# A backward pass of a gated spectral/GEGLU block: the real DFT over d split into even and odd d, joined and parted at the spectral filter

## The chip, the cores and the metric

One core of one Trainium2 chip. The metric is device time of one execution in microseconds (us). The kernel before takes 1464.88 us, the median of three runs (1464.13 to 1465.75).

## The reference, cut to what matters

S = 2048 rows, D = 576 columns, F = 4608, bf16 throughout. The kernel computes the forward output and all gradients of

```python
g = sigmoid((x * gate_w).sum(-1, keepdims=True))
a = irfft2(rfft2(x) * (w_r + 1j * w_i))                  # over (S, D): 2048 x 289 spectrum
b = (gelu(x @ w_gate) * (x @ w_up)) @ w_down
out = g * a + (1 - g) * b
# outputs: out, and d(out) . grad_out for x, w_r, w_i, w_gate, w_up, w_down, gate_w
```

So one 2-D real DFT is taken of x and one of g * grad_out; with W = w_r + i w_i the spectra give X W (for a), G conj(W) (for dx) and G conj(X) (for dw_r, dw_i); the first two are transformed back. The DFT over d gives 289 values of l for each row, each a sum over 576 d of x times cos and sin.

## The kernel before, in words

Everything that a DFT does is a matmul against a table of cosines and sines.

*Stage 0, the head* (before the loop over g). x and grad_out are loaded, transposed on TensorE in chunks (`tchunk`, L268 to 286) into xT and dOT (d on the partitions, five chunks: four of 128 d and one of 64). `build_D` (L95) makes the tables Dt: for each chunk of 128 d, cos and sin for all 289 l. `build_R` and `build_B` make the tables for the two halves of the DFT over s (2048 = 16 x 128). `fwd_units` (L476) gives 16 units u1 (over d: ten matmuls of 289 columns, L483, then an eviction by ACT, L487 or L489) and 16 units u2 (first half over s: four matmuls, L497 to L500, an eviction by DVE or ACT, L503/L505, a store). For x all 32 run in the head, on four PSUM tiles in turn; `gate` (L288) ends it.

*Stage 1, the loop over g* (18 blocks of 256 columns of F) and m (4 blocks of 512 rows): 72 steps. Each step runs `H_mm` (z = dO w_down^T, L312/L315; xy = x [w_gate w_up], L319/L324), the elementwise GEGLU and its derivative (`H_da`, `H_q`, `H_ew1`, `H_ew2`: ACT evicts and takes sigmoids, DVE does 24 operations per step on 128x512 bf16 tiles), and stores three results A, dHg, dHu to DRAM on SP's queue (L383). Between them stand the weight-gradient matmuls of the block g before (`W_units`, L417, L434, L447), evicted by `wevac`: every third by DVE, the others by ACT. `load_w` loads the next block's weights, one part at the end of each of the first three steps.

The rest of the spectral branch is a list `fft` of 174 slots, spread over the steps by `want` (L768): 4 slots in each of the first four steps, then 2.59 per step, evenly. The list: u1/u2 for grad_out; the filter stage `mid_units` (L535); two inverse transforms `inv_units` (L648). In the filter stage 16 rows i are taken in pairs p. s2 (L547) finishes the DFT over s: four matmuls and one ACT eviction into X or G. Then `products` (L569) puts DVE operations into the list `side`: two halvings, six products of 1156 elements (L583) and six sums and differences of 578 (L589/L590); three items of `side` are issued after each of a step's two elementwise tiles. s1 (L615) starts the way back: four matmuls, one ACT eviction, two stores. In `inv_units` z and ztail do the second half over s, d (L691) the transform over l: per row i and for cos and sin, two matmuls of 289 columns against Dt and one against the small table At2 for the last 33 l (L698, L700); ACT evicts, and DVE gives columns d from the sum and 576 - d from the difference of the two (L704, L705).

All spectral units in the loop share one PSUM tile with z (`pftile`, tag "z", one buffer). All small tiles (Y, Vt, Vp, W, X, G, products, ev, yo) share one pool of 19 buffers (`unit`).

*Stage 2*: the matmuls over F (L945) for b and dx, from A, dHg, dHu transposed back by DMA, with `post` and `x_end` on DVE; `gate_grad` (L988) sums dlog x over the 2048 rows by 80 one-column matmuls (L993).

The order of every engine's work is that in which the code issues it. SP's queue issues all loads and most stores in order; POOL's issues the stores of weight gradients from two `stage` buffers.

Of the kernel before, what the change touches and what calls it, by code (L numbers as in the profile page):

```python
# [9 lines left out]
ACT = mybir.ActivationFunctionType  # L10
# [30 lines left out]
NL = DF - 256  # L41
# [16 lines left out]
def iotas(nc, res, unit):  # L58
# [3 lines left out]
    tb.lrow = unit([DF], F32, name="lrow")  # L62
    G.iota(tb.lrow[:], pattern=[[1, DF]], base=0, channel_multiplier=0, **kw)
    tb.dcol = res.tile([P, 5], F32, name="dcol")
    G.iota(tb.dcol[:, 0:4], pattern=[[128, 4]], base=0, channel_multiplier=1, **kw)
# [10 lines left out]
    G.iota(tb.qcol_i[:], pattern=[[0, 1]], base=0, channel_multiplier=1)  # L76
    tb.halfpi = res.tile([P, 1], F32, name="halfpi")
# [17 lines left out]
def build_D(nc, tb, unit, res, c0, n):  # L95

    V = nc.vector
    step = 2.0 * math.pi / D
    TS = (nc.gpsimd if c0 else V).tensor_scalar
    X = unit([n, DF], F32, name="XD")  # L100
    y = unit([n, DF], F32, name="yD")
# [6 lines left out]
    o = unit([n, 2, DF], name="Dt")  # L108
    V.scalar_tensor_tensor(y[:], X[:], -1.0, X[:], op0=ALU.mult, op1=ALU.max)
    r = LO if c0 == 4 else slice(0, P)  # L110
    if c0 == 4:
        nc.gpsimd.memset(o[HI, :, :, :], 0.0)
    nc.scalar.activation(o[r, :, 0, :], y[r], ACT.Sin, bias=tb.halfpi[r], scale=-step)
    nc.scalar.activation(o[r, :, 1, :], X[r], ACT.Sin, scale=-step * EPS_SCALE)
    tb.Dt += [o[:, c] for c in range(n)]
# [51 lines left out]
def kernel(  # L167
# [25 lines left out]
    scr_x = dram.tile([T, P, 2, DF], BF16, name="scr_x")  # L193
    scr_g = dram.tile([T, P, 2, DF], BF16, name="scr_g")
    scr_p1 = (dram.tile([T, P, 2, 256], BF16, name="scr_p1"), dram.tile([2, T, P, NL], BF16, name="scr_q1"))
    scr_p2 = (dram.tile([T, P, 2, 256], BF16, name="scr_p2"), dram.tile([2, T, P, NL], BF16, name="scr_q2"))
# [7 lines left out]
    wts = {}  # L204

    def load_w(g, part):

        fsl = slice(g * FG, (g + 1) * FG)
        if part == 0:
            wgu = wpool.tile([P, 5, 2 * FG], BF16, tag="wgu", name="wgu")  # L210
            wdT = wpool.tile([P, 5, FG], BF16, tag="wdT", name="wdT")
            wts[g] = wgu, wdT
        wgu, wdT = wts[g]
        if part < 2:
            w, cols = (B_w_gate, B_w_up)[part], slice(part * FG, (part + 1) * FG)
            LD.dma_start(wgu[:, 0:4, cols], w[0:512, fsl].rearrange("(c p) f -> p c f", p=P))
            for r in (LO, HI):
                LD.dma_start(wgu[r, 4, cols], w[512:D, fsl])
# [127 lines left out]
    def H_ew1(xy, q):  # L346
# [6 lines left out]
        V.tensor_tensor(q[:], xb[:], q[:], op=ALU.mult)  # L353
        return xb, q, s, hu

    stores = []

    def flush(n=9):

# [735 lines left out]
```

## Time and profile before

| What | Value |
|---|---|
| median of three runs | 1464.88 us |
| profiled execution | 1460.16 us, span 1458.4 us, mean granted clock 0.997 |
| PE matmul / weight load | 1440.9 us / 1065.9 us |
| DVE, ACT, POOL | 845.7, 686.0, 120.3 us |
| head | 0 to 51.8 us |
| loop over g and m | 51.8 to about 1004 us, 72 steps |
| filter stage, s2 and s1 | 221 to 561 us |
| inverse transforms | 578 to 910 us |
| PE stops and waits | 10 us in all, 4.9 of them for the first load of x |

In a line of the profile, L312 is line 312 of the kernel; "out<-in" are tiles by the program's names; 128*128 128x289 is a matmul of 128x128 weights that writes 128 partitions by 289 columns. A matmul's own time includes the filling of the array, so its cost is read from the distance between the starts of two that follow each other. A stretch of the table of stretches gives, after its bounds and length, the busy time of each engine with the number of instructions, then the granted clock, the DMA engines' mean busy share and GB/s.

### The profile page before, as it was taken

The page shows a single profiled execution, that of the slowest core. Times are in us where ns is not written, and L with a number is a line of the kernel's source. Part 1 is how long each engine was busy: PE and PEld are TensorE (multiplying, and loading weights), DVE is VectorE, ACT ScalarE, POOL GpSimd, SP SyncE. Part 2 cuts the span into 40 slices and gives each one's busy share as a digit, 9 for nine tenths or more (in the row PEclk, how much of TensorE's full clock was granted, in tenths as well). Part 3 has the DMA queues.
Part 4 walks back from the last instruction along what each step waited for, and adds up shares of the span by engine and source line. Part 5 has one row for each costly group of instructions (what it writes and reads, how often), then busy time and mean ns, then how long its engine had stood idle before and what let it go on. Part 6 is the DMA issues. An engine that isn't in the chain of part 4 may idle for free.

```text
span 1458.4 us, 30071 instructions
## 1 busy us (share of the span) xinstructions
PE 1440.9 (99%) x11776; PEld 1065.9 (73%) x11776; DVE 845.7 (58%) x2256; ACT 686.0 (47%) x1354; POOL 120.3 (8%) x206
## 2 busy tenths in 40 slices
PE   8999999999999999999999999999999999999998
PEld 6766677767777677677677677768877777777776
DVE  7697677888887886777777777773000531212100
ACT  5776666766676666766766766662000000000000
POOL 2000011001011001001001001100000100000000
PEclk9999999999999999999999999999999999999998
DMA  5244344455445445434543544757999998878773
GB/s 192 68 122 120 115 130 120 137 146 143 138 139 150 117 119 138 125 110 113 143 127 102 139 127 118 176 135 172 255 197 198 218 198 166 165 159 169 149 149 72
DMA packets 501160, 210.54 MB, mean 144 GB/s; under 512 B 320950, under 2 KB 491128, under 8 KB 501016
## 3 DMA queue, kind: packets, MB, share of 16 engines
q1 hardware_dynamic: 491416, 188.10, 54.4%
q0 software_dynamic: 7792, 19.49, 4.3%
q8 instruction: 92, 1.51, 0.5%
q10 hardware_dynamic: 1808, 1.02, 0.3%
q14 instruction: 52, 0.43, 0.1%
HBM read 40.89 MB, written 93.82 MB: 92 GB/s over the span
## 4 chain that ended last, share of the span: by engine, by line
PE 92%; DVE 4%; ACT 1%; issue 1%; DMA 0%; DVEq 0%; ACTq 0%
PE acc L945 29%; PE wps L434 17%; PE xy L324 16%; PE wps L417 9%; PE z L312 8%; PE wps L447 2%; PE xy L319 2%; PE z L315 1%; PE pf L698 1%; PE pf L672 1%; PE pf L483 1%; PE pf L700 1%; PE fx L483 0%; DVE Vt L503 0%; DMA pin<-scr 0%
## 5 line engine op out<-in xcount | busy, mean ns | idle before, releaser
L945 PEld LDWEIGHTS <-pin 128*128 128x128 bf16 x3456 | 338.8, 98 | 87.0 <-DMA pin<-scr 1.0
L324 PE MATMUL xy<-wgu,xT 128*128 128x512 bf16 x1152 | 271.4, 380 | 0.0
L434 PEld LDWEIGHTS <-xn 128*128 128x128 bf16 x2304 | 225.3, 98 | 32.4 <-issue 0.2
L324 PEld LDWEIGHTS <-xT 128*128 128x128 bf16 x1152 | 106.8, 98 | 137.4 <-issue 30.4
L337 ACT ACTIVATE da<-z,omg 128x256 bf16<-128x256 f32 x288 | 113.4, 475 | 147.7 <-PE z L315 144.6
L962 ACT COPY bo<-acc 128x288 f32<-128x288 f32 x32 | 12.8, 399 | 308.9 <-PE acc L945 308.9
L417 PE MATMUL wps<-dB,A 128*128 128x288 bf16 x1152 | 154.2, 286 | 0.0
L945 PE MATMUL acc<-wgT,pin 128*128 128x288 bf16 x1152 | 145.3, 288 | 0.0
L945 PE MATMUL acc<-wuT,pin 128*128 128x288 bf16 x1152 | 143.6, 286 | 0.0
L945 PE MATMUL acc<-wd_all,pin 128*128 128x288 bf16 x1152 | 142.8, 286 | 0.7 <-DMA pin<-scr 0.7
L312 PE MATMUL z<-wdT,dOT 128*128 128x256 bf16 x1152 | 137.7, 273 | 1.7 <-ACT Y L489 1.2
L417 PEld LDWEIGHTS <-A 128*128 128x128 bf16 x1152 | 112.7, 98 | 35.7
L434 PE MATMUL wps<-dHg,xn 128*128 128x256 bf16 x1152 | 134.4, 273 | 0.0
L434 PE MATMUL wps<-dHu,xn 128*128 128x256 bf16 x1152 | 131.5, 273 | 0.0
L312 PEld LDWEIGHTS <-dOT 128*128 128x128 bf16 x1152 | 111.2, 98 | 19.1 <-issue 6.0
L1019 DVE SCALAR_TENSOR_TENSOR f32t<-gwf,dlog,b16t 128x576 f32<-128x576 f32 x16 | 13.1, 817 | 185.9 <-DMA b16t<-dxa_scr 185.9
L343 ACT ACTIVATE q<-xy 128x512 bf16<-128x512 f32 x144 | 86.1, 598 | 70.1 <-PE xy L324 65.8
L367 ACT ACTIVATE om<-s 128x512 bf16<-128x512 bf16 x144 | 92.0, 639 | 9.1 <-DVE s L351 8.9
L350 DVE TENSOR_SCALAR s<-q 128x512 bf16<-128x512 bf16 x144 | 42.8, 298 | 90.5 <-ACT q L343 88.4
L368 ACT ACTIVATE s<-s 128x512 bf16<-128x512 bf16 x144 | 90.7, 630 | 4.6
L440 POOL DMA_DIRECT2D out_dram<-dw x67 | 48.3, 721 | 534.3 <-ACT dw L395 256.7
L349 ACT CAST hu<-xy 128x512 bf16<-128x512 f32 x144 | 87.0, 604 | 0.0
(187 smaller groups left out, 1771.5 us busy)
## 6 DMA issues: line engine op xcount, KB each, us to landing
scr<-A SPq DMA_DIRECT2D x144, 128.0 KB, 2.2
scr<-dHg SPq DMA_DIRECT2D x144, 128.0 KB, 2.0
scr<-dHu SPq DMA_DIRECT2D x144, 128.0 KB, 2.1
out_dram<-dw POOLq DMA_DIRECT2D x67, 128.0 KB, 2.6
wd_all<-in_B_w_down_dram SPq DMA_DIRECT2D x3, 1728.0 KB, 15.0
out_dram<-dwd POOLq DMA_DIRECT2D x34, 144.0 KB, 2.2
wgu<-in_B_w_gate_dram SPq DMA_DIRECT2D x18, 256.0 KB, 3.1
wgu<-in_B_w_up_dram SPq DMA_DIRECT2D x18, 256.0 KB, 3.1
```

The costliest lines, as they stand in the source:

```text
L312: nc.tensor.matmul(zo(t), lhsT=dOT[:, ci, t, :], rhs=wdT[:, ci, :], start=(t % 4 < 2 and ci == 0), stop=False)
L324: nc.tensor.matmul(xy[k][:, t % 2, :], lhsT=xT[:, ci, t, :], rhs=wgu[:, ci, :], start=False, stop=(ci == 3))
L337: nc.scalar.activation(da[:, tt, :], z[:, tt, k, :], ACT.Copy, scale=omg32[:, t:t + 1])
L343: nc.scalar.activation(q[:], xy[:, :, 0:FG], ACT.Square)
L349: nc.scalar.copy(hu[:], xy[:, :, FG:2 * FG])
L350: V.tensor_scalar(s[:], q[:], A_GELU, 1.0, op0=ALU.mult, op1=ALU.add)
L367: nc.scalar.activation(om[:], s[:], ACT.Sigmoid, scale=-2.0 * C_GELU)
L368: nc.scalar.activation(s[:], s[:], ACT.Sigmoid, scale=2.0 * C_GELU)
L417: nc.tensor.matmul(wps[:, :288], lhsT=tl(0, t)[:, fch * P:(fch + 1) * P], rhs=dB[:, t, h * 288:(h + 1) * 288], start=(t == 0), stop=(t == ...
L434: nc.tensor.matmul(wps[:, cc, :], lhsT=xn[:, t, (c0 + cc) * P:(c0 + cc + 1) * P], rhs=tl(k, t), start=(t == 0), stop=(t == T - 1))
L440: wst[0].dma_start(ov[:, c0:c0 + TPB, fsl], dw[:])
L945: nc.tensor.matmul(acc[:, :288], lhsT=src[:, r, :], rhs=w_of(r)[:, h * 288:(h + 1) * 288], start=(first and r == 0), stop=(last and r == F ...
```

## The change

Since cos and sin of 2 pi l d / 576 keep their value or change their sign when l goes to l + 288, according to whether d is even or odd, an even and an odd sum over l = 0 .. 144 hold what 289 values held: with e and o the two, value l is e + o and value 288 - l comes from e - o (its imaginary part with the sign turned, and for row -k of the spectrum). The change carries every spectrum in that form up to the filter and from it.

- The transposes take every second column of d; tables have 145 columns (HF) instead of 289; u1 has six matmuls of 290 columns (even, odd, and one chunk of 64 d for both) instead of ten of 289. u2, s2, s1 keep four matmuls, of 290 columns.
- In s2 ACT evicts to f32 (`xe`), and two DVE operations of 290 and 288 elements write e + o and e - o, the latter backwards, into X and G.
- Since the second half of each spectrum row stands at row -k, w_r and w_i are copied in DRAM with their rows reversed (34 copies on POOL's queue at the end of the head, from DRAM to DRAM, 2 x 128 rows of 144 bytes each), POOL negates w_i's half, and the gradients of w are written to DRAM and copied back reversed (34 copies on SP's queue, three per step, after the last pair).
- `fold` turns each product back into e and o (four DVE operations of 576 elements per pair, half of them with a reversed input, and two small copies). The scaling by SD2 moves into `gs32`.
- d has, for cos and sin, two matmuls of 145 columns and one of 290; the table for odd d on the way back (`Oi`) is made by transposes in `tail_table`.
- `want` counts a slot of the filter stage as 1.7; while in that stage, `wevac` leaves DVE out. The A tiles have 13 buffers instead of 14.
- `load_w` loads w_gate and w_up in part 0, transposes w_down to `wtmp` in part 1 and copies it into wdT in the new order of d in part 2 (four more copies).
- `gate_grad`: DVE accumulates dlog x over the row blocks, and ten one-column matmuls remain.

```diff
+HF = 145
+NL = 2 * (HF - P)
+def eo(c):
+    return slice(256 * (c % 2) + c // 2, 256 * (c % 2) + 256, 2)
...
         elif part == 1:
+            wtmp[0] = wpool.tile([P, 4, FG], BF16, tag="wtmp", name="wtmp", bufs=1)
+            LD.dma_start_transpose(wts[g][1][:, 4:5, :], B_w_down[fsl, DCH[4][0]:D])
+            LD.dma_start_transpose(wtmp[0][:], B_w_down[fsl, 0:512])
         else:
+            wdT = wts[g][1]
             LD.dma_start(wdT[LO, 4, :], wdT[HI, 4, :])
+            for par in range(2):
+                for h, r in enumerate((LO, HI)):
+                    LD.dma_start(wdT[r, 2 * par:2 * par + 2, :], wtmp[0][par:P:2, h:4:2, :])
...
-    keepA = wstack.enter_context(tc.tile_pool(name="keepA", bufs=14))
+    keepA = wstack.enter_context(tc.tile_pool(name="keepA", bufs=13))
...
-                        nc.tensor.transpose(tp_[:, 0, j, tt, :], src[:, t0 + tt, c * P:(c + 1) * P], ident[:])
+                        nc.tensor.transpose(tp_[:, 0, j, tt, :], src[:, t0 + tt, eo(c)], ident[:])
...
-        if ectr[0] % 3 == 0:
+        if ectr[0] % 3 == 0 and not in_mid[0]:
             V.tensor_copy(out, in_)
...
-                for c, ci in [(c, ci) for c in range(2) for ci in range(4)] + [(0, 4), (1, 4)]:
-                    nc.tensor.matmul(yps[:, c, :DF], lhsT=src[:, ci, t, :], rhs=tb.Dt[ci][:, c, :],
-                                     start=(ci == 0), stop=(ci == 4))
+                for par, j in [(par, j) for par in range(2) for j in range(2)] + [(0, 2), (1, 2)]:
+                    ci, tab = (4, 4 + par) if j == 2 else (2 * par + j, 2 * par + j)
+                    nc.tensor.matmul(yps[:, par, :2 * HF], lhsT=src[:, ci, t, :], rhs=tb.Dt[tab].rearrange("p c l -> p (c l)"),
+                                     start=(j == 0), stop=(j == 2))
...
+    def reversed_rows(eng, src, dst):
+        s_, d_ = (a.rearrange("(m i) (h l) -> h i m l", i=T, h=2) for a in (src, dst))
+        return [lambda i=i: eng.dma_start(d_[:, i], s_[:, T - i, ::-1]) for i in range(1, T)] + \
+            [lambda: eng.dma_start(d_[:, 0, 1:P], s_[:, 0, P - 1:0:-1]), lambda: eng.dma_start(dst[0:1], src[0:1])]
...
-            LD.dma_start(w[:, 0], wr_v[:, i0:i0 + 2, :])
-            LD.dma_start(w[:, 1], wi_v[:, i0:i0 + 2, :])
+            for k, v in enumerate((wr_v, wi_v)):
+                LD.dma_start(w[:, k, :, 0:HF], v[:, i0:i0 + 2, 0:HF])
+                LD.dma_start(w[:, k, :, HF:DF], tiles_of(wrev[k])[:, i0:i0 + 2, :])
+            nc.gpsimd.tensor_scalar(w[:, 1, :, HF:DF], w[:, 1, :, HF:DF], -1.0, None, op0=ALU.mult)
...
-                if which == "x":
-                    nc.scalar.copy(o[:, ii], xps[:, :, :DF])
-                else:
-                    nc.scalar.activation(o[:, ii], xps[:, :, :DF], ACT.Copy, scale=SD2)
+                xe = unit([2, 2 * HF], F32, name="xe")
+                nc.scalar.copy(xe[:], xps[:, :, :w])
+                V.tensor_tensor(o[:, ii, :, 0:HF], xe[:, :, 0:HF], xe[:, :, HF:w], op=ALU.add)
+                V.tensor_tensor(o[:, ii, :, DF - 1:HF - 1:-1], xe[:, :, 0:HF - 1], xe[:, :, HF:w - 1], op=ALU.subtract)
...
+            def fold(key):
+                def f():
+                    m = st[p, key]
+                    q = unit([2, 2, 2, HF], name="q" + key)
+                    for e, op in enumerate((ALU.add, ALU.subtract)):
+                        V.tensor_tensor(q[:, :, :, e, 0:HF - 1], m[:, :, :, 0:HF - 1], m[:, :, :, DF - 1:HF - 1:-1], op=op)
+                    V.tensor_copy(q[:, :, :, :, HF - 1], m[:, :, :, HF - 1:HF].to_broadcast([P, 2, 2, 2]))
+                    st[p, key + "_q"] = q
+                return f
...
                 def store():
+                    for k, v in enumerate((o2v, o3v)):
+                        LD.dma_start(v[:, i0:i0 + 2, 0:HF], o[:, :, k, 0:HF])
+                        LD.dma_start(tiles_of(orev[k])[:, i0:i0 + 2, :], o[:, :, k, HF:DF])
+                    if p == T // 2 - 1:
+                        for k, v in enumerate((out_2, out_3)):
+                            moves.extend(reversed_rows(LD, orev[k][:], v[:, HF:DF]))
...
-                LD.dma_start(dst[0][i], Vt[:, :, 0:256])
-                LD.dma_start(dst[1][:, i].rearrange("c p l -> p c l"), Vt[:, :, 256:DF])
+                LD.dma_start(dst[0][i].rearrange("p c (e l) -> p c e l", e=2), Vt[:, :, :, 0:P])
+                for c in range(2):
+                    LD.dma_start(dst[1][c, i], Vt[:, c, :, P:HF])
...
                 for c in range(2):
-                    for lc in range(2):
-                        nc.tensor.matmul(yps[:, c, :DF], lhsT=Z[:, ii, 2 * lc + c, :], rhs=tb.Dt[lc][:, c, :],
-                                         start=(lc == 0), stop=False)
+                    for e, tab in enumerate((tb.Dt[0], tb.Oi)):
+                        nc.tensor.matmul(yps[:, c, e * HF:(e + 1) * HF], lhsT=Z[:, ii, 2 * e + c, :], rhs=tab[:, c, :],
+                                         start=(e == 0), stop=False)
...
+    for k, v in enumerate((A_w_r, A_w_i)):
+        for move in reversed_rows(nc.gpsimd, v[:, HF:DF], wrev[k][:]):
+            move()
...
+        def load(n):
+            return n + 0.7 * min(max(n - mid_at, 0), n_mid)
...
+            for _ in range(3):
+                if moves:
+                    moves.pop(0)()
...
+            V.scalar_tensor_tensor(gacc[:], xn[:, t, :], dlog[:, t:t + 1], gacc[:], op0=ALU.mult, op1=ALU.add)
...
-                for t in range(T):
-                    nc.tensor.matmul(gps[0:n, c:c + 1], lhsT=xn[:, t, c * P:c * P + n], rhs=dlog_bf[:, t:t + 1],
-                                     start=(t == 0), stop=(t == T - 1))
+                for v in range(2):
+                    nc.tensor.matmul(gps[0:n, c:c + 1], lhsT=gsplit[:, v, c * P:c * P + n], rhs=ones[:],
+                                     start=(v == 0), stop=(v == 1))
```

## The prediction

> **What bounds the kernel now.** I read the busy shares first, then the chain of work that ended last, then the table of stretches, then PE's timeline for the pace of one matmul. Busy shares and chain:
>
> ```profile
> PE 1440.9 (99%) x11776; PEld 1065.9 (73%) x11776; DVE 845.7 (58%) x2256; ACT 686.0 (47%) x1354; POOL 120.3 (8%) x206
> PE 92%; DVE 4%; ACT 1%; issue 1%; DMA 0%; DVEq 0%; ACTq 0%
> ```
>
> TensorE is busy 99% of the span and is 92% of the chain. "PE busy" is an extent and not a pace, so the table of stretches has to confirm it. Its columns are the stretch, its length, then busy PE, PEld, DVE, ACT, POOL:
>
> ```profile
> 11.10:49.80 38.70, 38.08 (x385) 29.85 (x386) 25.71 (x60) 25.45 (x42) 0.00 (x0) 1.00 0.38 115
> 63.40:94.20 30.80, 29.39 (x200) 17.85 (x200) 28.77 (x78) 25.69 (x49) 0.00 (x0) 1.00 0.47 133
> 94.20:122.50 28.30, 27.29 (x224) 19.22 (x224) 26.90 (x80) 19.84 (x38) 1.81 (x3) 1.00 0.36 102
> 252.80:570.60 317.80, 317.62 (x2539) 225.63 (x2538) 267.72 (x707) 215.54 (x430) 30.57 (x48) 1.00 0.50 137
> 1104.00:1430.00 326.00, 325.96 (x2661) 260.39 (x2662) 72.20 (x169) 7.99 (x20) 24.21 (x44) 1.00 0.86 173
> ```
>
> See three things. From 122 us on PE never rests. VectorE has much room in the last stage, 16% room in the filter stage (252.8 to 570.6 us, where spectra are multiplied), and almost none from 63 to 122 us. There PE does lose time: 0.8 us of z waiting for ACT's Y, 0.9 us of L483 waiting for DVE's Vt. So a matmul removed is time removed, except where DVE is already full.
>
> **Prices on PE**, from its timeline (start, extent, line):
>
> ```profile
> 15.93 1.05 PE L275 MATMUL tp<-ident,xn 128*128 128x128 bf16 x16
> 16.92 0.41 PE L278 MATMUL tp<-ident,xn 128*64 128x128 bf16 x8
> ...
> 21.24 1.40 PE L483 MATMUL fx<-Dt,xT 128*128 128x289 bf16 x10
> 22.48 0.28 PE L497 MATMUL fx<-Y,Rt 128*128 128x289 bf16 x1
> ...
> 49.77 2.14 PE L292 MATMUL fx<-gwT,xT 128*128 128x1 bf16 x80
> 51.77 1.91 PE L312 MATMUL z<-wdT,dOT 128*128 128x256 bf16 x16
> ...
> 902.52 0.41 PE L698 MATMUL pf<-Dt,ZT 128*128 128x289 bf16 x2
> 902.77 0.29 PE L700 MATMUL pf<-At,ZU 66*128 66x289 bf16 x1
> ```
>
> Start to start: ten matmuls of 289 columns take 1.24 us, 124 ns each; sixteen of 128 columns 0.99 us, 62 ns; eighty of one column 2.00 us, 25 ns. The last shows that a weight load costs at most 25 ns of pace, so halving the columns does halve a matmul.
>
> **What goes from PE.** (a) u1, forward over d: 10 matmuls become 6, in 32 units: 32 x 4 x 0.124 = 15.9 us, half of it in the head (before 49.8 us), half in 56 to 171 us. (b) d, inverse: four of its six matmuls go from 289 to 145 columns. 145 columns cost 62 ns (half of 124) to 70 ns (62 x 145/128); I take 64: 32 x 4 x 0.060 = 7.7 us. (c) gate_grad: 80 one-column matmuls become 10, priced like L292: 1.75 us. Back: one column more on some 600 matmuls (0.4 ns each, 0.25 us) and eight transposes in tail_table (0.4 us). **Sum: 24.7 us.** The head's transposes now load every second column; even at double the 25 ns, that load stays under the 62 ns pace.
>
> **What is added, and what covers it.**
>
> *DVE in the filter stage.* Per pair p (8 slots): s2 now unfolds on DVE, 8 tensor_tensors of 290 f32, like L704 (458 ns): 3.7 us. fold adds twice two bf16 tensor_tensors of 576, one input of one of them read backwards, and a copy of 8 (0.17). No row reads bf16 backwards; the bounds are L589 (578 bf16, 460 ns) and L979 (576 f32, 752 ns): 2.2 to 3.4 us. The products remain: by their rows 7.65 us. So 7.65 becomes 13.5 to 14.7. A plain step (the last four, 948.5 to 995.5 us) has 9.05 us of DVE, a step of the filter stage 267.72/24 = 11.15 in 13.24, thus 2.1 us of products per step, at 2.59 slots per step 6.5 us per pair: overlap makes it 85% of the rows' sum. The new want() gives the stage 2.0 slots a step (4 steps per pair) and moves the wevac third (0.45 us a step) to ACT: 8.6 + 14.7 x 0.85/4 = 11.7 us of DVE in a step that PE needs 12.9 for (0.6 slots of 0.5 us fewer): 91%, against 84%. Two steps in four are heavier: products come six a step, so some 13 us against 12.4. The q, s, hu and da buffers of two and three tiles let DVE trail by most of a step, and step 291.8 to 306.7 had DVE at 14.14 of 14.90 with PE at 14.76. I charge 2 us (0 to 10). ACT takes those evictions at 9.0 of 13.2 us (an f32 eviction, L703, costs 653 ns, the bf16 one, L560, 643): covered.
> Two waits are new on DVE. The unfold waits for ACT's copy of s2; behind it stand sig1's tile and ACT's sigmoids of it, and DVE waits there only when it is ahead. With 13 A buffers the second tile of m = 2 waits for PE's dwd reads of the g before; behind it stand dHg and dHu. DVE runs that tile after PE has passed, so nothing; without that cover 1 us in each of 17 g.
> The Trainium skill, "VectorE: DVE Perf Modes", section "Mode 2×_1P — pack two bf16 into one 32-bit read", grants two results a cycle at a step of +1 or -1, with 4-byte alignment. L589 and L590 disagree on the alignment: rows starting at 578 bytes run as fast. By that page fold stands, as an estimate, at 2.2 us per pair, and the 2 us charged become about 1.
>
> *The head.* PE's 38.08 us fall to about 30.2, DVE's 25.7 and ACT's 25.5 stay (83%); u2 waits for ACT's Y with 1.24 us of PE work between instead of 1.74, and one copy behind one sine is 0.64 + 0.62. I charge 1 us (0 to 3), 1 us for the tail_table copies ahead of the gate (0 to 2), and credit 0.5 for half-width tables. In the last stage 16 ops like L976 (818 ns) are nothing: DVE has 72 busy of 326 us.
>
> *63 to 122 us.* DVE had 55.7 of 59.1 us and loses nothing; u1 would save 4 to 5 us there, 3.4 is all the room. Charge 2.5 us (0.5 to 4.5).
>
> *Denser slots outside the filter stage*, 3.4 instead of 2.59 a step through the one z bank: the four-slot steps lost 0.8 and 0.4 us on z behind ACT. Charge 1 us (0 to 4).
>
> *SP and the DMAs.* SP gets about 12 more issues in four steps (wdT's four part copies, halves of W and of the outputs, a third s1 store): 0.4 to 0.6 us each, 6 of 52 us, on a queue half full. What waits behind them: wdT for the next g, a full step ahead of its z, and the p+1 spectra, whose tightest case is the first pair, one slot (7 us) ahead, landing in 4: maybe 1 us. POOL's negations hold its stores of dw behind the W loads; two stage buffers cover that. The 34 wrev copies run on POOL from 8 us on, needed after 180. The 34 orev copies go three per step; the first waits on SP for the last stores to land (3 us), with a step's stores behind it. Packets of 66, 132 and 256 bytes took 12, 14 and 18 ns in the trace's packet records, so 256 rows of 144 bytes are 0.2 us spread over sixteen engines, or 1.8 us each if only two take part. No row copies DRAM to DRAM. Charge 0.5 us (0 to rival 2).
> The Trainium skill, "DMA: Bandwidth & Descriptors", section "Why a DMA increments its semaphore by 16 and not by 1", speaks against this copy: the number of engines is the largest up to 16 that divides the slowest dimension, here h = 2, so two engines. By it, three copies a step would add an estimated 5.4 us to those two, still under what is free; the sum stays.
>
> **Sum.** 24.7 - 2 - 1 - 1 + 0.5 - 2.5 - 1 - 0.5 = 17.2 us. The profiled execution took 1460.16 us (span 1458.4): 1443.0. The three runs have a median of 1464.88, 4.7 above it; by the same step, **1447.7 us**.
>
> **Rivals.**
> 1. *VectorE becomes the bound of the filter stage.* For: 91% on average, heavier in pairs of steps, and DVE must now wait in order for s2's eviction before it goes on with sig1. Against: PE stayed full at 95%. If the rows add without overlap, 8.6 + 14.75/4 = 12.3 us, and a wait of 1 us a step makes 13.3 against 12.9: 35 steps x 0.4 = 14 us lost instead of 2, 1460. Between, 1453 to 1462. It cancels the change at 0.7 us per step.
> 2. *Slower: the orev copies clog two DMA engines and SP.* Place: the dozen steps after the filter stage. The engines are 50% busy, so about 6.5 us a step are free; three copies of 128 packets need 0.384 t. At 14 ns: 5.4, covered. From t = 17 ns a backlog starts; SP's transfers queue behind it and z waits for wdT once 11 us of lead are gone. To eat 17 us as well takes 28 us over 11.3 steps: t = 23 ns; that is where it decides. At 30 ns: 11.3 x (11.5 - 6.5) - 11 = 46 us, so 1465 - 17 + 46 = 1494.
> 3. *Nothing is lost:* buffers ride out 63 to 122 us and the filter stage: 24 to 26 us, 1440.
>
> **How the numbers follow.** Forecast (12 to 24 us, 1441 to 1453) 0.62; rival 1 at 1453 to 1462, 0.16; rival 3, 0.08; rival 2, 0.08; DVE so late that it costs more than it saves, 0.03; even, 0.03. Differences under 0.2% (2.9 us) can't be told from none here. Faster 0.84, same 0.05, slower 0.11. Range 1438 to 1461: it leaves out rival 2 and the ends.
>
> **What would show it.** PE: x11586, u1's line six matmuls per 0.75 us, d's six in 0.50. The filter stage's steps at 12.9 us with DVE near 11.7. PE waits on DVE below 3 us after 122 us. Fold's rows at 460 to 750 ns. SP's orev copies landing in 2 to 6 us, and no PE wait on wdT; such a wait, or steps of over 13.5 us in the filter stage, would prove me wrong.

## The result and the profile after

The changed kernel takes 1498.47 us (median of four, 1496.51 to 1502.81), the kernel before on the same chip 1464.51 us: a ratio of 1.0235 (1.0212 to 1.0259). It is 34 us slower; the forecast was 17 us faster, and 1498 lies 37 us above the top of the range.

The profiled execution (1496.51 us, span 1494.7) shows on its page the busy shares, three rows of its 40 slices, and the chain:

```profile
PE 1414.5 (95%) x11500; PEld 1050.8 (70%) x11586; DVE 887.8 (59%) x2356; ACT 697.2 (47%) x1380; POOL 172.1 (12%) x258
...
PE   4388999999999999998999999999999999999997
...
PEclk8699999999999999999999999999999999999998
DMA  9925454455565555446556546665999998878773
...
PE 77%; DVE 2%; issue 1%; DMA 0%; SPq 0%; ACT 0%; DVEq 0%
```

TensorE is busy 26 us less, and the span is 36 us longer. (86 matmul records are missing from this trace; the weight loads count the 11586 that were forecast.) The first three slices (37 us each) tell where: PE at 4, 3 and 8 tenths, the DMA engines at 9, 9 and 2. Three stretches of the two kernels, from the first instruction to the first z, from there to the last stage, and the last stage, measure 51.8, 943.7 and 462.9 us before, and 87.1, 943.6 and 464.0 after. So 35.3 of the 36.3 us are lost in the head. The loop came out even although by the forecast's prices its matmuls ask 15.4 us less (7.95 for u1, 7.7 for d, 0.25 back), so it lost as much to other things.

PE's waits over the whole run, costliest first (what waited, for whom; total, times, longest):

```profile
PE fx L530 <- ACT Y L519: 35.7, 4, 29.2
...
PE z L341 <- DMA wdT<-wtmp: 4.4, 2, 3.8
```

The large one leads from u2 to ACT's copy Y, so the next view is what ACT waited for before 87 us, and then SP's timeline from 8 us on (start, length, line, transfer), first in the changed kernel, then two rows of the kernel before:

```profile
ACT Rt L152 <- DMA scr_x<-Vt: 28.1, 1, 28.1
```

```profile
11.88 8.04 SPq L238 DMA_DIRECT2D wgu<-in_B_w_up_dram  x2
19.97 3.62 SPq L241 DMA_TRANSPOSE wdT<-in_B_w_down_dram  x1
23.64 4.16 SPq L242 DMA_TRANSPOSE wtmp<-in_B_w_down_dram  x1
...
39.25 6.83 SPq L248 DMA_DIRECT2D wdT<-wtmp  x4
46.18 13.12 SPq L541 DMA_DIRECT2D scr_x<-Vt  x7
```

```profile
14.87 1.21 SPq L220 DMA_TRANSPOSE wdT<-in_B_w_down_dram  x1
...
19.87 18.07 SPq L506 DMA_DIRECT2D scr_x<-Vt  x10
```

SP works in order. Its loads and transposes of W take two to three times as long as before (a transpose 3.62 us, before 1.21), so the first store of scr_x is issued at 46.18 us (before 19.87). ACT's sine needs a unit tile that such a store still holds, the Y copies stand behind the sine, and PE behind Y. The table of stretches gives the state of the chip then (stretch, length, busy PE, PEld, DVE, ACT, POOL; granted clock, DMA share, GB/s):

```profile
15.00:20.00 5.00, 5.00 (x41) 3.79 (x40) 2.46 (x5) 3.47 (x6) 2.34 (x3) 0.63 1.16 161
...
25.00:30.00 5.00, 4.62 (x51) 3.45 (x48) 3.99 (x11) 2.42 (x4) 1.33 (x3) 1.00 1.35 41
30.00:35.00 5.00, 0.00 (x0) 0.10 (x1) 0.71 (x2) 0.00 (x0) 2.78 (x3) 0.73 1.22 56
35.00:40.00 5.00, 0.00 (x0) 0.00 (x0) 0.00 (x0) 0.00 (x0) 1.44 (x3) 0.50 1.24 47
```

From 25 us on the DMA engines count as more than full (packets that overlap in time count each) and move 41 to 56 GB/s; from 30 us on TensorE, VectorE and ScalarE stand nearly or quite still. Only POOL works: it issues the 34 wrev copies, from 8.5 to 70 us. In the packet records, SP's packets of 512 bytes between 10 and 60 us fall into two kinds: three quarters took 28.5 ns on average, and 24% took over 60 ns, with a mean of 422. Before, the mean was 31.6, and none took over 52. This reads as if something sat on some of the engines at a time, and each transfer of SP waited for its slowest packets; the experiments test the first half of it.

The rows that answer to the stretches shown of before (63 to 94 us, 94 to 122, the filter stage, the last stage), same columns:

```profile
98.70:128.80 30.10, 26.10 (x173) 15.39 (x176) 28.50 (x76) 25.46 (x49) 0.00 (x0) 1.00 0.52 141
128.80:157.70 28.90, 26.91 (x220) 19.00 (x222) 27.04 (x81) 20.41 (x39) 1.92 (x3) 1.00 0.49 131
286.30:640.00 353.70, 347.76 (x2764) 247.93 (x2797) 311.04 (x846) 246.43 (x493) 49.03 (x68) 1.00 0.56 134
1139.70:1466.20 326.50, 326.49 (x2670) 260.82 (x2671) 84.00 (x171) 7.98 (x20) 23.94 (x44) 1.00 0.87 173
```

In the first row VectorE has 28.50 of 30.10 us and PE rests for 4. The first two stretches together are as long as before (59.0 us, before 59.1), so what u1 saves there became waiting in a stretch in which VectorE is full.

### The profile page after: what moved, and what is told of

The parts are those of the page before. It is cut to its first block, busy times and chain, and to the rows that moved or that the text cites. A ratio compares the mean times of both kernels' runs of the same rounds, so it can differ in the third digit from the quotient of the medians.

```text
span 1494.7 us, 30032 instructions
## 1 busy us (share of the span) xinstructions
PE 1414.5 (95%) x11500; PEld 1050.8 (70%) x11586; DVE 887.8 (59%) x2356; ACT 697.2 (47%) x1380; POOL 172.1 (12%) x258
## 4 chain that ended last, share of the span: by engine, by line
PE 77%; DVE 2%; issue 1%; DMA 0%; SPq 0%; ACT 0%; DVEq 0%
PE acc L1043 28%; PE wps L464 14%; PE xy L353 12%; PE wps L447 8%; PE z L341 7%; PE wps L477 2%; PE xy L348 2%; PE z L344 1%; PE pf L745 1%; PE pf L772 1%; PE pf L774 1%; DMA pin<-scr 0%; PE pf L695 0%; PE pf L696 0%; PE pf L698 0%
## 5 line engine op out<-in xcount | busy, mean ns | idle before, releaser
L353 PE MATMUL xy<-wgu,xT 128*128 128x512 bf16 x1066 | 257.9, 380 | 10.1 <-issue 8.3
L341 PE MATMUL z<-wdT,dOT 128*128 128x256 bf16 x1152 | 141.1, 277 | 7.0 <-DMA wdT<-wtmp 4.4
L1120 DVE SCALAR_TENSOR_TENSOR f32t<-gwf,dlog,b16t 128x576 f32<-128x576 f32 x16 | 13.1, 817 | 179.2 <-DMA b16t<-dxa_scr 179.2
```

Of the source, the lines that this page charges most:

```text
L341: nc.tensor.matmul(zo(t), lhsT=dOT[:, ci, t, :], rhs=wdT[:, ci, :], start=(t % 4 < 2 and ci == 0), stop=False)
L353: nc.tensor.matmul(xy[k][:, t % 2, :], lhsT=xT[:, ci, t, :], rhs=wgu[:, ci, :], start=False, stop=(ci == 3))
```

## Experiments

Theory 1: the wrev copies hold DMA engines, wherever they are issued. Theory 2: SP's own new issues for wdT hold it. Theory 3: the head needs more unit tiles and waits for them in any case. Times are medians; "kernel before" is the one run beside each, 1462.4 to 1464.5 us. Stages, steps and waits are those of one profiled execution, which can lie some us from the median. Steps are counted from 0.

### Which part holds the head

**e1_wrev_late.** POOL issues the copies after the gate.

```diff
-    for k, v in enumerate((A_w_r, A_w_i)):
-        for move in reversed_rows(nc.gpsimd, v[:, HF:DF], wrev[k][:]):
-            move()
     x2[T - 1]()
     gate()
+    nc.gpsimd.tensor_copy(after_gate[:], gs32[:])
+    for k, v in enumerate((A_w_r, A_w_i)):
+        for move in reversed_rows(nc.gpsimd, v[:, HF:DF], wrev[k][:]):
+            move()
```

> Theory 1 (the 34 wrev copies hold the DMA engines in the head, so SP's loads and the stores of scr_x land late): with the copies issued by POOL after the gate instead of from 8 us on, the first z moves from 87 us back to 50 to 57 us, SP's packets in the head fall from a mean near 122 ns to 20 to 40 ns, and the time falls by 25 to 35 us to 1462 to 1472; part of the price may come back in the first steps of the loop, where the copies now lie. Theory 2 (SP's own new issues for wdT stand ahead of the scr_x stores): the first z stays above 75 us and the time above 1485. Theory 3 (more unit tiles in the head, so ACT waits for a free one in any case): as theory 2.

Measured: 1493.35 us; first z at 51.4 us, and step 3 of the loop takes 39.16 us where it took 9.97. The head recovered as theory 1 says, and the time, forecast at 1462 to 1472, did not: 29 us of the head's 35 came back in that one step. Most of the price moved along with the copies. PE's longest wait from 50 to 125 us, and SP's timeline under it:

```profile
PE z L341 <- DMA wdT<-wtmp: 30.0, 1, 30.0
```

```profile
95.52 3.91 SPq L241 DMA_TRANSPOSE wdT<-in_B_w_down_dram  x1
99.49 3.45 SPq L242 DMA_TRANSPOSE wtmp<-in_B_w_down_dram  x1
...
118.39 1.48 SPq L245 DMA_DIRECT2D wdT<-wdT  x1
120.39 2.65 SPq L248 DMA_DIRECT2D wdT<-wtmp  x4
```

SP is late as in the head of the changed kernel, here with wdT for the next g.

**e3_wdT_late.**

```diff
-    for part in range(3):
+    for part in range(2):
         load_w(0, part)
 ...
+    load_w(0, 2)
     build_B(nc, tb, unit, res)
```

> wdT's five copies of g = 0 go behind the scr_x stores in SP's order; the wrev copies stay. Theory 2 (those copies hold SP): first z at 50 to 57 us, time 1462 to 1472. Theory 1 (the wrev copies congest the DMA engines): the stores of scr_x start some 10 us earlier but still land late, the first z stays at 70 to 87 us, and the time falls by no more than 15 us, to 1482 to 1497.

Measured: 1497.09 us, first z at 77.7 us. Theory 2 falls: the time is that of the changed kernel. (The first z in this execution, the fastest of four, came 9 us earlier than in the changed kernel's; in e5 and e15 below, whose head is the changed kernel's to the letter, it comes at 82.6 and 88.5 us.)

**e4_before_wrev.** The kernel before, with `reversed_rows` and its loop; nothing reads wrev.

```diff
     tail_table()
+    for k, v in enumerate((A_w_r, A_w_i)):
+        for move in reversed_rows(nc.gpsimd, v[:, 145:DF], wrev[k][:]):
+            move()
     x2[T - 1]()
```

> The kernel before with nothing new but the 34 wrev copies on POOL at the same place, their result unused. Theory 1: these copies alone delay the head: the first z goes from 52 us to 65 to 87 us and the time up by 13 to 35 us, to 1478 to 1500. Theories 2 and 3: nothing of the new wdT path or of the new unit tiles is here, so the time stays within 3 us of the kernel before, 1462 to 1468.

Measured: 1489.80 us, ratio 1.0175 (1.0160 to 1.0190); first z at 74.7 us, and the later steps take what they took in the kernel before, within 0.5 us. Theories 2 and 3 fall as the cause: the copies alone, added to the old kernel, cost 26 us, 22.9 of them in the head. Why the changed kernel's head lost 12 us more was not taken apart.

### What makes the copies dear

Theory A: POOL's software queue. Theory B: the copy's outermost dimension of two. Theory C: reading the rows backwards. The Trainium skill, "DMA: Bandwidth & Descriptors", section "Why a DMA increments its semaphore by 16 and not by 1", says that a transfer goes to as many engines as the largest number up to 16 that divides the slowest dimension of source and target, here two.

**e6_wrev_sp.** The copies on SP's hardware queue, four a step.

```diff
-        for move in reversed_rows(nc.gpsimd, v[:, HF:DF], wrev[k][:]):
-            move()
+        moves.extend(reversed_rows(LD, v[:, HF:DF], wrev[k][:]))
 ...
-            for _ in range(3):
+            for _ in range(4 if pr < 12 else 3):
                 if moves:
```

> The 34 wrev copies go on SP's hardware queue, four at the end of each step from the first step of the loop on, as the orev copies do; all of them stand ahead of the first load of the W tiles. Theory A (the price belongs to POOL's software queue: there the copies stretch everybody's packets; by the hardware queue a 144-byte packet takes 16 to 22 ns): first z at 50 to 57 us, SP's other packets in 50 to 150 us below 45 ns on average, at most 10 us lost to SP's issue time (four issues of 1.2 us a step), time 1455 to 1475. Theory B (two engines and small rows from DRAM to DRAM, by any queue): z waits for wdT by some 30 us in the first nine steps and the time stays at 1485 to 1500.

Measured: 1487.49 us; z waits 26.1 us for wdT, in six pieces, 7.0 of them at the orev copies, which are those of the changed kernel. Hardly any packets are stretched (512 bytes: 29 ns on average), but a copy holds SP for about 1.9 us (the medians of its two rows are 2.1 and 1.8), and the transfer behind four of them for 2.2 to 2.6 more. SP's timeline:

```profile
72.49 6.64 SPq L587 DMA_DIRECT2D wrev<-in_A_w_r_dram  x4
79.67 2.33 SPq L541 DMA_DIRECT2D scr_g<-Vt  x1
```

128 packets of 144 bytes at the median of 14 ns that they took here are 1.8 us, about the time for which SP is held (at the mean, 22 ns, they are 2.8). So the copies are dear on the hardware queue too, in another way: they hold SP, and do not stretch the packets of others. That POOL's queue alone is the cause, theory A, falls.

**e8_fwd2** and **e12_fwd16_144** leave out the reversal and keep 256 rows of 144 bytes on POOL; they differ in the outermost dimension. **e7_fwd16** has 128 rows of 288 bytes.

In short, with the target on the left (the loops and the rest of the calls are left out):

```text
 e8:  w_[:, i] <- r_[:, i]   with "(m i) (h l) -> h i m l", h=2
 e12: w_[i] <- r_[i]         source "(m i) (h l) -> i m h l", target laid out "(h m i l)"
 e7:  w_[i] <- r_[i]         with "(m i) l -> i m l"
```

> The wrev copies stay on POOL from 8 us on with the outermost dimension of two and rows of 144 bytes, but in forward order (the rows are not reversed, so the products after them have other values). If the backward step of the source is what costs: first z at 50 to 60 us, time 1458 to 1470. If it is the shape or the queue: as the changed kernel, first z at 75 to 90 us, time 1485 to 1500.

> The wrev copies stay on POOL from 8 us on and keep 256 rows of 144 bytes each, but the rows (128) are the outermost dimension and not the two halves; the order is forward (rows not reversed and laid out in halves, so the products after them have other values). Theory two engines (an outermost dimension of two puts a copy on two of sixteen engines): the head recovers, first z at 52 to 60 us, time 1462 to 1472. Theory packets (twice as many rows of half the length as in the forward copy with 288 bytes is what costs): first z at 70 us or later, time over 1480.

> The wrev copies stay on POOL from 8 us on, but copy 128 rows of 288 bytes in their order, with the rows as the outermost dimension (the rows are not reversed, so the products after them have other values): half the rows, all sixteen engines by the page. Theory B (two engines per copy are the bottleneck): the head recovers, first z at 50 to 60 us, time 1458 to 1470. Theory A (the software queue itself, whatever the shape): first z at 65 us or later, time over 1475.

Measured: e8 1495.30 us (first z 86.3), e12 1472.86 (57.1), e7 1467.23 (53.7). e8 and e12 have the same bytes, the same number of rows and the same queue: with two outermost the head is lost, with 128 outermost 29 us of it come back. The rows of the tile wrev, first the changed kernel, then e12 (length of an issue, first and last start; time to land):

```profile
L587 POOL DMA_DIRECT2D wrev<-in_A_w_r_dram x15: 1064/1067/1237, 8.5 to 34.1; - x15
L587 POOL DMA_DIRECT2D wrev<-in_A_w_i_dram x15: 1064/1064/1095, 40.4 to 66.3; - x15
```

```profile
L824 POOL DMA_DIRECT2D wrev<-in_A_w_r_dram x16: 686/686/717, 8.4 to 21.6; - x16
L824 POOL DMA_DIRECT2D wrev<-in_A_w_i_dram x16: 686/686/688, 22.3 to 32.8; - x16
...
DMA to landing us min/median/max: 2.9/6.2/7.5
```

The queue is done at 33 us instead of 70, and 2% of SP's 512-byte packets take over 60 ns instead of 24% (28% in e8). Theory B stands, theory C falls: e8 reads its rows forwards and is as late as the changed kernel. The page's rule agrees with all three. The packet records carry no engine, but their sizes show the parts: a copy is ten packets in the changed kernel (eight of 4176 bytes and two of 1728, which is twice 4 x 29 + 12 rows) and sixteen of 2304 bytes (16 rows) in e12. Added up, these packets took 140 us in the changed kernel and 130 in e12, so the amount is nearly the same and its spread is what differs. Whether it is the few engines or the longer packets that hold up the others, these runs do not separate: an outermost dimension of two brings both.

### The orev copies, and what is left without any

**e5_no_orev** takes the first line below away, **e15_orev16** puts the two others in its place.

```diff
-                            moves.extend(reversed_rows(LD, orev[k][:], v[:, HF:DF]))
+                            r_, w_ = (a.rearrange("(m i) l -> i m l", i=T) for a in (orev[k][:], v[:, HF:DF]))
+                            moves.extend([lambda i=i, r_=r_, w_=w_: LD.dma_start(w_[i], r_[i]) for i in range(T)])
```

> The 34 orev copies are left out, so the second halves of out_2 and out_3 are not written; all else is as in the changed kernel. If SP, held by three copies per step, made PE wait for wdT near 710 us: that wait (4.4 us) and the step's loss of 6.8 us go, the time falls by 5 to 8 us to 1488 to 1493, and the head stays as late as it is. If that loss had another cause (a lower clock, the scheduler's denser slots): no more than 2 us.

> As the changed kernel, but the orev copies on SP have the 128 rows as outermost dimension, 288 bytes each, in forward order (rows of out_2 and out_3 past column 144 land unreversed). Read at steps 47 and 48, where the changed kernel loses 6.8 us. If two engines per copy hold SP (three issues in 4 to 6 us): an issue falls to about 0.5 us, the wait for wdT goes, those steps fall from 34 us to 27 to 28. If three more issues a step on SP cost by their number: the steps stay above 31 us. The head stays late: time 1485 to 1493.

Measured: e5 1489.59 us, e15 1491.74; steps 47 and 48 take 27.4 us in both (34.2 in the changed kernel). Three issues a step are harmless; with two outermost they are not. The rows for the orev copies, changed kernel and then e15:

```profile
L587 SPq DMA_DIRECT2D out_dram<-orev x30: 605/1170/2222, 635.6 to 775.6; - x30
```

```profile
L676 SPq DMA_DIRECT2D out_dram<-orev x32: 497/596/693, 637.6 to 767.8; - x32
```

**e9_no_copies.** No wrev and no orev; both loops of copies are gone as well.

```diff
-                LD.dma_start(w[:, k, :, HF:DF], tiles_of(wrev[k])[:, i0:i0 + 2, :])
+                LD.dma_start(w[:, k, :, HF:DF], v[:, i0:i0 + 2, HF:DF])
 ...
-                        LD.dma_start(tiles_of(orev[k])[:, i0:i0 + 2, :], o[:, :, k, HF:DF])
+                        LD.dma_start(v[:, i0:i0 + 2, HF:DF], o[:, :, k, HF:DF])
```

> No wrev and no orev copies: the second halves of W are loaded from, and those of out_2 and out_3 stored to, the rows k instead of -k (the reversal is left out). If everything in the prediction but the copies held: 1443 to 1450. By the two traces, which show 35 us lost in the head, 7 at the orev copies, and some 8 to 12 us more than forecast in the opening steps, at 299 us and at the end: 1453 to 1460.

Measured: 1455.43 us, ratio 0.9939 (0.9924 to 0.9955): by the medians 8 us faster than the kernel before, by the profiled executions 5.2 (1454.98 against 1460.16), where 17.2 were forecast from that execution. Head, loop and last stage: 51.7, 938.2 and 463.3 us. The head gained next to nothing from 8 us of matmuls less. PE's waits there, up to 53 us:

```profile
PE tp L303 <- DMA xn<-in_A_x_dram: 5.0, 1, 5.0
PE fx L530 <- ACT Y L519: 3.4, 3, 1.9
PE z L341 <- ACT g_bf L322: 1.4, 1, 1.4
PE fx L514 <- DVE Dt L133: 1.1, 1, 1.1
PE tp L306 <- DVE Vt L538: 0.8, 1, 0.8
```

6.7 us of waiting behind the first line, against 1.8 before. After the early ones PE's next 5.7 us, from 13.75 us on, run at about half pace as well (work of some 3.1 us by the later rows; sixteen transposes in 1.85 us where others take 0.98), though the granted clock in the table of stretches is 1.00 there.

**e11_gather_end**: W by gathers, the outputs by scatters on rows -k (below), build_B at t = 13, and gate_grad one job earlier.

```diff
+        if t == 13:
+            build_B(nc, tb, unit, res)
 ...
-    build_B(nc, tb, unit, res)
 ...
+            if i == len(jobs) - 2:
+                gate_grad()
```

> The gathers and scatters, and two pieces moved: gate_grad's ten matmuls and its store come one job earlier (ahead of the second half of dx for t = 14), and build_B's tables come at t = 13 of the head instead of behind it. If the store of dgw, 16 us to land, ends the run: the last stage falls by 3 to 5 us. If the head ends with the sines of build_B and the table load ahead of the gate's sigmoid: the first z comes 1 to 2.5 us earlier. Together 4 to 7 us below the kernel with gathers alone: 1448 to 1453. If neither: the same time as that kernel within 1.5 us.

Measured: 1468.93 us against 1471.40. The head's part held (first z 50.3 us). The end's did not: the last stage takes 468.3 us, and PE waits 8.1 us for pin. SP's timeline shows two rounds of six transposes, without and with the dgw store (issued at 1426) beside them:

```profile
1401.73 16.11 SPq L984 DMA_TRANSPOSE pin<-scr  x6
...
1419.37 28.27 SPq L984 DMA_TRANSPOSE pin<-scr  x6
```

The store of 576 elements of two bytes is dear there too, for those beside it.

**e14_no_copies_row**: e9 with build_B early and gate_grad as one row.

```diff
-                    nc.tensor.matmul(gps[0:n, c:c + 1], lhsT=gsplit[:, v, c * P:c * P + n], rhs=ones[:], ...)
+                    nc.tensor.matmul(gps[0:1, :288], lhsT=ones[:], rhs=gsplit[:, v, hs], ...)
 ...
+            ST.dma_start(out_7.rearrange("(o d) -> o d", o=1), dgw[0:1])
```

> The kernel without any reversal (rows k in place of rows -k in W's and the outputs' second halves), with build_B's tables at t = 13 of the head, and gate_grad as four matmuls of 288 columns into one row, stored by one DMA of 1152 bytes instead of two of two-byte elements. If the 16 us that the two-byte store takes to land are the tail of the run: the last stage falls by 3 to 6 us and the first z comes 1 us earlier: 1449 to 1452 against 1455 without these two. If the tail is set by something else (the last block's own store): 1453 to 1456.

Measured: 1446.05 us, 3 us below the range; first z at 50.2, last stage 456.4. From PE's last matmul to the end of the span it takes 3.2 us, 10.4 in the changed kernel, and 6.2 before: the store had cost the old kernel 3 us too.

### Reversed rows without the copies

**e10_gather.** An index table of -k; 32 gathers and 32 scatters on POOL, 128 rows of 288 bytes each.

```diff
+    nc.gpsimd.iota(neg[:], pattern=[[-1, T]], base=S, channel_multiplier=-T)
+    nc.vector.tensor_single_scalar(neg[:], neg[:], S - 1, op=ALU.bitwise_and)
 ...
-                LD.dma_start(w[:, k, :, HF:DF], tiles_of(wrev[k])[:, i0:i0 + 2, :])
+                for ii in range(2):
+                    nc.gpsimd.indirect_dma_start(w[:, k, ii, HF:DF], None, (A_w_r, A_w_i)[k], row_of(i0 + ii), element_offset=HF)
```

> No wrev and no orev: the second halves of the W tiles come by 32 indirect gathers of rows -k, those of out_2 and out_3 go by 32 indirect scatters, 128 rows of 288 bytes each, all on POOL, in the order in which the pairs use them. If only the two-engine copies cost the time: the time of the kernel without any reversal, 1453 to 1458, below the kernel before. If small transfers on POOL's queue cost by themselves, about 1 us each as the wrev copies did: 64 of them, 25 us and more, spread over the filter stage, 1475 to 1490.

Measured: 1471.40 us, between the two. Up to step 13 its steps are e9's; then some 13 us go in steps 14 to 36: scatters to one output wait on POOL for each other's landing, and VectorE for the tile that they read (7.8 us in one piece).

**e13_gather_tiles.** Scatters into a scratch tensor per tile, from there 32 forward copies on SP, two a step; build_B and gate_grad as in e14.

```diff
-                            nc.gpsimd.indirect_dma_start((out_2, out_3)[k], row_of(i0 + ii), o[:, ii, k, HF:DF], None, element_offset=HF)
+                            nc.gpsimd.indirect_dma_start(orow[k][i0 + ii][:], bass.IndirectOffsetOnAxis(ap=rev_u[:, c:c + 1], axis=0),
+                                                         o[:, ii, k, HF:DF], None)
 ...
+                            rows = v[:, HF:DF].rearrange("(m i) l -> i m l", i=T)[(T - i) % T]
+                            moves.append(lambda rows=rows, k=k, i=i: LD.dma_start(rows, orow[k][i][:]))
```

> The full computation: W's second halves by gathers; the outputs' second halves scattered into one scratch tensor per tile (so that no scatter waits for another one's landing) and moved on by SP with the 128 rows outermost, two a step; build_B early and gate_grad as one row as in the kernel without reversal. If the 9 us that the gathers and scatters cost over no reversal came from scatters waiting for each other on POOL, with VectorE waiting for their tile: within 3 us of the kernel without reversal, 1450 to 1455. If gathers cost by themselves: 1457 to 1463.

Measured: 1455.67 us, ratio 0.9953 (0.9940 to 0.9967): what it loses to e14 in the profiled executions is 7.6 us in steps 16 and 17, 1.1 in step 0, 1.3 in the head and 2.1 in the last stage. VectorE's wait from 240 to 290 us, and POOL's timeline:

```profile
DVE qm L673 <- DMA orow<-o,rev: 7.1, 1, 7.1
```

```profile
255.51 1.06 POOL L680 TENSOR_SCALAR o<-o 128x288 bf16<-128x288 bf16 x1 [15.98 <-DVE o L664]
...
265.06 1.13 POOL L617 TENSOR_SCALAR Wt<-Wt 128x288 bf16<-128x288 bf16 x1 [1.94 <-DMA Wt<-in_A_w_i_dram,neg]
...
267.28 1.05 POOL L687 DMA_INDIRECT orow<-o,rev  x1 [0.30 <-issue]
```

The tile is ready at 256.5; the scatter stands behind the next pair's gathers and leaves at 267.

**e16_scatter_now** issues the scatters right behind the negation at L680 (first hunk: the call moves there from `store`). **e17_side_two** is e16 with the second hunk: two products per half step.

```diff
                 nc.gpsimd.tensor_scalar(o[:, :, 1, HF:DF], o[:, :, 1, HF:DF], -1.0, None, op0=ALU.mult)
+                nc.gpsimd.indirect_dma_start(orow[k][i0 + ii][:], ...)
 ...
             def side_work():
-                for _ in range(3):
+                for _ in range(2):
```

> The kernel with gathers and per-tile scatters, but the scatters are issued by POOL right behind the negation of o instead of with the deferred stores. VectorE's 7.1 us wait for the unit buffer of o near 270 us should go: steps 16 and 17 fall from 37.2 us to 29 to 31, the time from 1455.7 to 1447 to 1450. If POOL's queue only passes the delay on to the gathers of the next pair, VectorE waits for W instead: steps 16 and 17 stay over 34 us and the time over 1453.

> As the kernel with early scatters, with two products taken per half step instead of three (four a step instead of six; a pair's 12 fit in 4 steps). If step 17 (16.7 to 17.1 us where its neighbours take 12.5 to 12.9) is late because VectorE gets too many products in a row: it falls to 12.5 to 14 us and the time by 3 to 4.5 us more, to 1443 to 1446. If the forced pops ahead of s1 bring the same work in worse places: new waits of PE on ACT's da or Vt, the time the same or up to 10 us longer.

Measured: e16 1450.06 us, ratio 0.9902; that wait is gone, but VectorE then waits 3.4 us for a unit tile that a scr_q store holds, so steps 16 and 17 take 33.5 us and not 29 to 31. e17: **1443.15 us, ratio 0.9858 (0.9841 to 0.9874)**, step 16 12.51 us and step 17 12.98, with the whole computation. Its page:

```profile
PE 1416.4 (98%) x11580; PEld 1046.9 (73%) x11580; DVE 885.0 (61%) x2356; ACT 696.8 (48%) x1382; POOL 203.3 (14%) x289
...
PE   6989999999999999999999999999999999999999
```

Not all of e17's 20.7 us below the kernel before belong to the change: the early tables and the one-row gate_grad, which the forecast did not contain and which have nothing to do with even and odd d, were worth 8 to 9 us from e9 to e14.

## Why the prediction was wrong

In this table, in us, the stages of the profiled spans stand beside the forecast's terms, sorted into them.

| stage | before | changed | no copies (e9) | e17 | forecast gain | gain of e9 |
|---|---|---|---|---|---|---|
| to the first z | 51.8 | 87.1 | 51.7 | 51.1 | 6.05 | 0.1 |
| loop | 943.7 | 943.6 | 938.2 | 931.3 | 9.4 | 5.5 |
| last stage | 462.9 | 464.0 | 463.3 | 457.8 | 1.75 | -0.4 |
| span | 1458.4 | 1494.7 | 1453.2 | 1440.2 | 17.2 | 5.2 |

The last stage of one and the same code differs by 4 us between executions (462.9 us here before, 467 in e4), so -0.4 there is no measure.

**The step that failed** is "the 34 wrev copies run on POOL from 8 us on, needed after 180". The sum has nothing for them in the head (0.5 us stand for SP and all DMAs), and the head lost 35.3 us: the first z came at 87.1 us with the copies and at 51.7 without (e9). The step asked when their result is wanted, and not whose transfers share the engines with them. A price stood two sentences further: 1.8 us each if only two engines take part. 34 of them are 61 us, and POOL's queue ran from 8.5 to 70; that the two agree so well is in part luck, since POOL's queue moved the rows in packets of up to 29 and not one by one. In that stretch SP has W, wdT and the scr_x stores to move, and the stores hold the tiles that ACT needs. The skill's rule on the outermost dimension was weighed in the prediction, but for orev alone, where 6.5 us a step were thought free.

**Rival 2** (the orev copies on two engines) named the right kind of copy and the right wait, but at the smaller of the two places where such copies run, and with the wrong size: 6.8 us were lost, not 28 or 46. A packet of 144 bytes took 16 ns in the median and 22 on average, close to the 23 at which the rival decides; by its own sum 22 ns would cost 11 us, and 16 nothing. Not a backlog of packets decided, as far as the trace shows, but SP's issue, and the sign that the prediction named for it, a wait of z on wdT, came. SP's and PE's timelines:

```profile
696.57 3.93 SPq L587 DMA_DIRECT2D out_dram<-orev  x3
...
707.02 2.63 SPq L248 DMA_DIRECT2D wdT<-wtmp  x4
```

```profile
709.90 0.58 PE L341 MATMUL z<-wdT,dOT 128*128 128x256 bf16 x2 [3.81 <-DMA wdT<-wtmp]
```

Three issues take 3.93 us, the stores behind them come late, and L248 is issued at 707.02, when PE has already been waiting for a microsecond. "A full step ahead" held for the order of the code, not for the queue. e5 and e15 show that the loss goes with the copies and with their shape.

**PE's savings** came as worked out: six matmuls of u1 start to start in 0.75 us, d's six in 0.51 (PE's timeline, changed kernel):

```profile
20.82 0.91 PE L514 MATMUL fx<-Dt,xT 128*128 128x290 bf16 x6
21.57 0.66 PE L530 MATMUL fx<-Y,Rt 128*128 128x290 bf16 x4
```

```profile
695.98 0.23 PE L772 MATMUL pf<-Dt,ZT 128*128 128x145 bf16 x1
...
696.36 0.29 PE L774 MATMUL pf<-At,ZU 68*128 68x290 bf16 x1
696.49 1.89 PE L353 MATMUL xy<-wgu,xT 128*128 128x512 bf16 x8
```

**The head's 1 us** for VectorE and ACT should have been 7: e9's first z comes at 51.7 us with 8 us of matmuls less. PE waited 4.9 us longer there and lost some 2.6 to the half pace after its waits. The reading is that a busy PE hid a chain of ACT and VectorE that was as long; no run shortens that chain alone (in e14 the tables, taken earlier, bring the first z from 51.7 to 50.2 us).

**The opening steps**, charged 2.5: steps 0 to 4 take 57.1 us and took 57.0, though about nine u1 units of 0.5 us are cheaper. So the charge was some 4.5 us, the upper end of what was allowed.

**The filter stage** (charged 2, and rival 1): its plain steps are 12.51, 12.51, 12.94 and 14.05 us, 13.0 on average for 12.9 forecast, with VectorE busy 45 to 46 of the 52.0 us of four, 11.4 a step for 11.7 forecast. Rival 1's loss in every step did not come. One step, number 17, lost about 4, because products came six a step; the prediction had named these heavier steps, and e17 shows that spacing them removes the loss (18.15 us in e16, 12.98 in e17). Fold's bf16 operations, read backwards, took 460 ns, its lower bound:

```profile
L660 DVE TENSOR_TENSOR qm<-m x16: 455/460/465, 272.8 to 614.8; 128x576 bf16<-128x576 bf16 x16
```

That agrees with the Trainium skill, "VectorE: DVE Perf Modes", section "Mode 2×_1P — pack two bf16 into one 32-bit read", which grants a step of -1 the same two results a cycle as a step of +1.

**gate_grad** saved its 1.7 us of matmuls (the last piece of the chain is 17.76 us, before 19.43) and gave them back: the copy of dgw stands on VectorE behind L1120, which waits for dxa; the store leaves at 1475.5 and lands 17 us later, behind everything else; the span ends 10.4 us after PE's last matmul (before 6.2).

What stays open: which engines POOL's queue uses, always the same two or others from copy to copy, which the records do not tell; why the copies cost the changed kernel's head 12 us more than that of the kernel before; and what in the opening steps could give VectorE room.

## What to carry to other kernels

Before a transfer is called hidden, ask which DMA engines it holds, for how long in all, and whose transfers need those same engines then; its own deadline says nothing about that. A copy whose outermost dimension is two was dear on both queues tried here: on POOL's, 34 of them delayed the head by 35 us where 32 with 128 outermost (e12) delayed it by 5, and on SP's one held the queue for 1.2 to 2.1 us where one with 128 outermost held it for 0.6. Where rows must be turned around, a gather or a scatter by an index table did it for 1.0 us of POOL each, as long as nothing had to wait for a scatter's landing. And when work is taken from the engine that looks full, look for the chain of the others that is just as long.

## What was not expected of the hardware

- A copy of 36 KB from DRAM to DRAM landed after 13.7 us (median) with two outermost, and after 6.2 us with 128 outermost (there with 36 KB too, rows in order), both on POOL's queue; through SP the first kind held the queue for about 1.9 us in e6 and 1.2 for orev, the second for 0.6 (e15, rows of 288 bytes).
- The store of 576 two-byte elements landed after 17 us, and six transposes beside it took 28.27 us instead of 16.11.
- PE's granted clock went to 0.50 in the stretches in which it stood still, and the z that followed a wait of 4 us ran slowly, with 0.50 granted from 709.9 to 714.3 us: fourteen of its matmuls spread over 3.17 us, where sixteen took 1.9 before.
- 128 rows of 288 bytes by an index table: 1.0 us of POOL each; the scatters into scratch tensors landed after 2.6 us (e17).
